# Large tiles laid out anew in on-chip memory, and the first and last copies cut in two, in an attention and gated-MLP kernel

## The chip, the cores and the metric

The kernel runs on one core of a Trainium2 chip. The metric is device time in microseconds (us) of one launch: 688.56 us is the median of three runs of the kernel before (688.14 to 688.83). The engines are named as in the profile: PE is TensorE (matmuls), PEld its weight loads, DVE is VectorE, ACT is ScalarE, POOL is GpSimd, SP issues all the transfers (DMAs).

## What is computed

Attention with a sigmoid in place of the softmax, and behind it a gated MLP whose gate mixes the positions of a sequence. The reference, cut to what matters:

```python
scores = scale * q @ k.T - log(S)          # 8 batches, 12 heads, S = 448, head size 64
attn = sigmoid(scores) @ v                 # heads side by side: x is (8, 448, 768)
h = maximum(x @ w_in, 0)                   # w_in: 768 x 1024
u, v = h[..., :512], h[..., 512:]
v_n = (v - mean(v)) / sqrt(var(v) + 1e-6)  # over the 512 features
v_s = w_spatial @ v_n + b_spatial          # over the 448 positions
out = (u * v_s) @ w_out                    # w_out: 512 x 768
```

## The kernel before

The batches are taken in four pairs (`m` = 0 to 3). For each pair the PE runs, in program order:

- **psc** (`attention_scores`, L237 and L225): scores of one pair of heads. A tile of 128 keys is the stationary operand (the weights, loaded by PEld), 448 queries stream past it. Queries and keys are split into a high and a low float32r part, and three products (`TERMS`) are summed. The short last tile of keys of two units goes in plain float32 (L225, `t == NFULL`). ACT turns the sums into `at` (sigmoid, L245).
- **pav** (`attention_values`, L267): `v` is stationary (64 columns for each of two heads, side by side in the array), `at` streams, in plain float32. The sums are split into the two parts of `x_s`.
- **pv** (`gate_values`): `x_s` is stationary, 512 columns of `w_in_s` stream. Then come the statistics, and the normalised tiles `vn`.
- **pg** (`spatial`): `vn` is stationary, 448 columns of `w_sp_s` stream.
- **pu** (`gated`): the u half of `w_in_s` is stationary, 448 columns of `x_s` stream. The product with the gate is split into two parts, `gs`.
- **po** (`output`): `w_out_s` is stationary, 448 columns of `gs` stream. ACT copies the sums to `osb` (L416) and SP sends them out (L417).

All of pv, pg, pu and po go through one helper, `product` (its matmul is L278), with float32r operands of 128 rows, and each matmul has a weight load of 128 columns of its own. The matmuls of the program number 504 (pv), 352 (pg), 576 (pu) and 576 (po).

Each engine's order is the order of the code (`in_program_order`). Transfers all go through SP's queue in that order: `start_loads` issues the first ones, and `attention` issues the rest a few steps ahead.

Where a tile lies is settled by the pools. A pool lays its tiles one after another in the order of their first use, each rounded up to 32 bytes, with all buffers of a tag together: `small`, then `const` (the weights, `b_bc` and `x_s`), then `work` (`raw`, `v`, `tmp`, `big`, `split`, `wval`). The tile `fill` (608 bytes) is used by nothing; it makes `w_in_s` begin at byte 2048 of each partition. All large tiles have sizes that are multiples of 256 bytes, so before the change all of them begin at multiples of 512.

At the **beginning** PE runs seven matmuls of zeros into `idle` (L478) while the first data come. The first unit's queries and keys come in two transfers (`pieces`): 640 columns with the 128 keys of the first tile, the queries and the short keys, then the 256 other keys. `attention_splits` makes the two parts: ACT copies the 576 columns of the first piece (L103), DVE subtracts (L104); DVE does both for the second. At the **end** the sums of the last two blocks of 128 outputs lie in one tile of two PSUM banks; one copy of 2 x 448 columns and one transfer send them out.

Of the kernel before, what the change touches and what calls it, by code (L numbers as in the profile page):

```python
# [8 lines left out]
F32 = mybir.dt.float32  # L9
F32R = mybir.dt.float32r  # L10
# [4 lines left out]
P = 128  # L15
# [20 lines left out]
def attn_gmlp_kernel(  # L36
# [25 lines left out]
    nc = tc.nc  # L62
    B, NHP, _, _ = qk.shape
    S = out.shape[3]
    D = P // 2
    NCC = out.shape[1]
# [4 lines left out]
    NFULL = 3  # L71

    REST = NFULL * P
    PART = REST + S
# [4 lines left out]
    small = ctx.enter_context(tc.tile_pool(name="small", bufs=2))  # L79
    const = ctx.enter_context(tc.tile_pool(name="const", bufs=1))  # L80
    work = ctx.enter_context(tc.tile_pool(name="work", bufs=2))

    ps_2 = ctx.enter_context(tc.tile_pool(name="ps_2", bufs=3, space=bass.MemoryType.PSUM))
    ps_1 = ctx.enter_context(tc.tile_pool(name="ps_1", bufs=2, space=bass.MemoryType.PSUM))
# [7 lines left out]
    table = small.tile([P, 1], F32, name="table", bufs=1)  # L92
    nc.scalar.activation(table, bias_s, AF.Sigmoid)

    small.tile([P, 152], F32, name="fill", bufs=1)

    w_in_s = const.tile([P, 2 * NCC, 2, F], F32R, name="w_in_s")
    w_out_s = const.tile([P, NFC * DM // 512, 2, 512], F32R, name="w_out_s")
    w_sp_s = const.tile([P, 4, 2, 512], F32R, name="w_sp_s")
    b_bc = const.tile([P, 512], F32, name="b_bc")  # L100
    x_s = const.tile([P, 2, NCC, 2 * S], F32R, name="x_s")
    def split(hi, lo, src, copy):
        copy(hi, src)  # L103
        nc.vector.tensor_sub(lo, src, hi.bitcast(F32))  # L104

    def banks(name):
        return ps_2.tile([P, 2, 512], F32, tag="ps2", name=name)
# [71 lines left out]
    def load_weights(n):  # L179
        for _ in range(n):  # L180
            next(weights, None)

    loaded = {}
    values = {}

    def pieces(b, hp, end):

        cut = REST - P
        return [slice(cut, end), slice(0, cut)] if b == hp == 0 else [slice(0, end)]

    def attention_loads(b, hp):
        raw = work.tile([P, 1024], F32, tag="raw", name=f"raw_{b}_{hp}", bufs=4)[:, : 2 * S]
        for cols in pieces(b, hp, 2 * S):
            nc.sync.dma_start(raw[:, cols], qk[b, hp, :, cols])
        loaded[b, hp] = raw

    def value_loads(b, hp):
        vt = work.tile([P, 2 * NFULL + 1, P], F32, tag="v", name=f"v_{b}_{hp}", bufs=3)
        nc.sync.dma_start(vt, v[b, hp // 2])
        values[b, hp] = vt  # L200

    parts_of = {}

    def attention_splits(b, hp):
        raw = loaded[b, hp]
        s = work.tile([P, 2, PART], F32R, tag="split", name=f"qks_{b}_{hp}", bufs=3)
        for i, cols in enumerate(pieces(b, hp, PART)):
            scalar = b == 1 or b == 0 and hp not in (1, 2) and i == 0
            split(s[:, 0, cols], s[:, 1, cols], raw[:, cols], nc.scalar.copy if scalar else nc.vector.tensor_copy)
        parts_of[b, hp] = s  # L210

    TERMS = ((0, 0), (1, 0), (0, 1))
# [61 lines left out]
    def product(ps, pairs, more=(), start=True, stop=True):  # L274

        ops = [(st(a), mv(c)) for st, mv in pairs for a, c in TERMS] + list(more)
        for i, (st, mv) in enumerate(ops):
            nc.tensor.matmul(ps, st, mv, start=start and i == 0, stop=stop and i == len(ops) - 1)  # L278
# [109 lines left out]
            hidden[b, fc] = gs[:, :, i]  # L388

    sums_of = {}  # L390

    def output(b, es, part=None):

        if not part:
            sums_of[es] = banks(f"po_{b}_{es[0]}")
        po = sums_of[es]
        n = NFC // 2
        for i, e in enumerate(es):

            def weight(a, fc, e=e):  # L400
                block, col = divmod(fc * DM + e * P, 512)
                return w_out_s[:, block, a, col : col + P]

            product(
                po[:, i, :S],
                [
                    (lambda a, fc=fc: weight(a, fc), lambda c, fc=fc: hidden[b, fc][:, c])
                    for fc in (range(NFC) if part is None else range(part * n, (part + 1) * n))
                ],
                start=not part,  # L410
                stop=part != 0,
            )
        if part == 0:
            return
        osb = work.tile([P, 2, 512], F32, tag="tmp", name=f"osb_{b}_{es[0]}", bufs=3)[:, :, :S]
        nc.scalar.copy(osb, po[:, :, :S])  # L416
        nc.sync.dma_start(out[b, es[0] : es[0] + 2].rearrange("e p s -> p e s"), osb)  # L417

    units = [(b, hp) for b in range(B) for hp in range(NHP)]
# [1 line left out]
    def ahead(f, n):  # L421
        if n < len(units):
            f(*units[n])

    def start_loads(m):
        n = m * 2 * NHP
        ahead(attention_loads, n)
        ahead(attention_loads, n + 1)
        ahead(value_loads, n)
        ahead(attention_loads, n + 2)  # L430

    def attention(m):

        first, end = 2 * NHP * m, 2 * NHP * (m + 1)
        waiting = []

        def scores(n, tiles):
            for t in tiles:
                if t == 1:
                    ahead(attention_splits, n + 1)  # L440
                if n + 2 < end and t == NFULL + 1:
                    ahead(attention_splits, n + 2)
                waiting.append((*units[n], t, attention_scores(*units[n], t)))
                if n + 2 < end:
                    if t == 0:
                        ahead(attention_loads, n + 3)
                        ahead(value_loads, n + 2)
                    elif t == NFULL and n + 4 < end:
                        ahead(attention_loads, n + 4)
                if m == 0 and (n > first or t > NFULL) and t != 2:  # L450
                    load_weights(1)

        def sums(n):
            for args in waiting[:n]:
                attention_values(*args)
            del waiting[:n]

        attention_splits(*units[first])
        yield
        for n in range(first, end, 2):  # L460
            for t in range(NFULL):
                scores(n, [t])
                if n == first:
                    yield
            scores(n, [NFULL])
            sums(NFULL + (n > first))
            scores(n, range(NFULL + 1, TILES))
            sums(len(waiting) - NFULL - 1)
        sums(NFULL + 1)

    start_loads(0)
    load_weights(1)

    zeros = work.tile([P, 512], F32R, tag="big", name="zeros", bufs=7)
    nc.vector.memset(zeros.bitcast(F32), 0.0)  # L475
    idle = banks("idle")
    for _ in range(7):
        nc.tensor.matmul(idle[:, 0], zeros[:, :P], zeros, start=True, stop=True)  # L478

    pairs = [(0, 1), (2, 3)]  # L480
    outs = [(0, 1), (2, 3), (4, 5)]
    running = attention(0)
    for m in range(B // 2):
# [14 lines left out]
        for fcs in pairs:  # L498
            spatial(b1, fcs)
            load_weights(BLOCK)  # L500
        start_loads(m + 1)
        for es in outs:
            output(b0, es)
# [14 lines left out]
        for part in range(2):  # L518
            for es in early:
                output(b1, es, part)  # L520
        for es in outs[len(early) :]:
            output(b1, es)
# [53 lines left out]
```

## Time and profile before

| | before |
|---|---|
| median of three runs | 688.56 us |
| time of the profiled execution | 688.86 us |
| its span, first to last instruction | 687.1 us |
| PE busy | 681.0 us (99%), 3839 instructions |
| PEld busy | 504.9 us (73%) |
| DVE, ACT busy | 292.7 us (43%), 241.2 us (35%) |
| DMA | 55.37 MB, mean 81 GB/s |

The profiled execution is one launch with the hardware profiler on. Its time is its span and 1.8 us around it. A float32 matmul stands as two instructions in the profile, so pav counts 768 for 384 products. PE's matmuls are pipelined: the duration of one (365 ns) reaches beyond the start of the next, and what counts is the distance from start to start, which the rows of the chain of waits give when a long piece of one kind is divided by its count.

### The profile page before, as it was taken

Reading aid. Unit: us, or ns where it says so; the run is one execution under the profiler, and the core shown is the slowest. Engines: PE = TensorE matmul, PEld = TensorE weight load, DVE = VectorE, ACT = ScalarE, POOL = GpSimd, SP = SyncE. Lnnn points to the kernel's source line nnn. Section 1 sums busy time; section 2 is a strip of 40 time slices with the busy share of each in tenths; the row PEclk is TensorE's granted clock in tenths of the full one; section 3 lists DMA queues with packets and bytes.
Section 4 is the critical chain, followed back from the end, with each engine's and each line's share of the span. In section 5 each row is a group of like instructions: output and inputs, shape, how many; then the busy total and the mean of one; then the engine's idle time right before and its main releaser. Section 6 shows DMA issues by size and latency. Waiting matters only on the chain.

```text
span 687.1 us, 9085 instructions
## 1 busy us (share of the span) xinstructions
PE 681.0 (99%) x3839; PEld 504.9 (73%) x3839; DVE 292.7 (43%) x469; ACT 241.2 (35%) x284; POOL 18.5 (3%) x36
## 2 busy tenths in 40 slices
PE   9999999999999999999999999999999999999997
PEld 5444789998554488999854458899984555889996
DVE  6999888803143237221233514721223241563010
ACT  6887010112567510011367651011137773101111
POOL 0000010000000001000000001100000000110000
PEclk9999999999999999999999999999999999999999
DMA  8873202230444100003062500000315310000102
GB/s 311 290 259 98 93 1 88 82 135 27 159 136 150 39 1 0 1 28 107 28 204 96 158 28 0 1 1 27 108 55 188 122 41 1 0 1 0 54 28 80
DMA packets 20392, 55.37 MB, mean 81 GB/s; under 512 B 1920, under 2 KB 8192, under 8 KB 20352
## 3 DMA queue, kind: packets, MB, share of 16 engines
q1 hardware_dynamic: 20352, 54.80, 23.4%
q8 instruction: 30, 0.49, 0.3%
q14 instruction: 10, 0.08, 0.0%
HBM read 43.78 MB, written 11.01 MB: 80 GB/s over the span
## 4 chain that ended last, share of the span: by engine, by line
PE 99%; ACT 0%; DVE 0%; issue 0%
PE pav L267 20%; PE po L278 17%; PE pu L278 17%; PE pv L278 17%; PE psc L237 15%; PE pg L278 10%; PE psc L225 3%; PE idle L478 0%; ACT osb L416 0%; DVE zeros L475 0%; DVE bias_s L88 0%; DVE mhalf L90 0%
## 5 line engine op out<-in xcount | busy, mean ns | idle before, releaser
L245 ACT ACTIVATE at<-psc,bias_s 128x896 f32<-128x896 f32 x168 | 158.6, 1008 | 60.8 <-PE psc L237 58.4
L267 PE MATMUL pav<-at,v 128*64 128x448 f32 (+1 forms) x768 | 139.4, 546 | 0.0
L278 PE MATMUL po<-gs,w_out_s 128*128 128x448 f32 x576 | 118.6, 366 | 0.0
L278 PE MATMUL pu<-x_s,w_in_s 128*128 128x448 f32 x576 | 118.0, 365 | 0.0
L278 PE MATMUL pv<-w_in_s,x_s 128*128 128x512 f32 x504 | 115.4, 390 | 0.0
L278 PEld LDWEIGHTS po<-gs,w_out_s 128*128 128x128 f32 x576 | 107.9, 188 | 9.7 <-ACT at L245 0.9
L278 PEld LDWEIGHTS pu<-x_s,w_in_s 128*128 128x128 f32 x576 | 108.2, 188 | 8.5
L278 PEld LDWEIGHTS pv<-w_in_s,x_s 128*128 128x128 f32 x504 | 94.3, 188 | 22.3 <-issue 2.8
L237 PEld LDWEIGHTS psc<-qks 64*128 64x128 f32 x864 | 77.2, 186 | 39.5 <-ACT at L245 15.5
L267 PEld LDWEIGHTS pav<-at,v 128*64 128x64 f32 (+1 forms) x768 | 44.0, 135 | 82.2 <-issue 76.5
L237 PE MATMUL psc<-qks 64*128 64x448 f32 x864 | 103.2, 379 | 0.2
L104 DVE TENSOR_TENSOR x_s<-pav,x_s 128x448 fp32r<-128x448 f32 x48 | 29.6, 623 | 125.6 <-ACT x_s L103 125.6
L278 PE MATMUL pg<-w_sp_s,vn 128*128 128x448 f32 x352 | 72.7, 365 | 0.0
L278 PEld LDWEIGHTS pg<-w_sp_s,vn 128*128 128x128 f32 x352 | 66.1, 188 | 5.4
L378 DVE SCALAR_TENSOR_TENSOR g<-pu,g 128x896 f32<-128x896 f32 x16 | 17.4, 1090 | 121.3 <-PE pu L278 121.3
L416 ACT COPY osb<-po 128x896 f32<-128x896 f32 x24 | 21.8, 907 | 119.9 <-PE po L278 111.7
L103 ACT CAST gs<-g 128x896 fp32r<-128x896 f32 x16 | 15.1, 942 | 129.9 <-DVE g L378 129.9
L104 DVE TENSOR_TENSOR qks<-raw,qks 128x832 fp32r<-128x832 f32 (+2 forms) x49 | 49.3, 1007 | 4.6 <-ACT qks L103 3.2
L298 ACT ACTIVATE rv<-pv 128x1024 f32<-128x1024 f32 (+1 forms) x16 | 14.8, 922 | 100.8 <-PE pv L278 93.0
L103 DVE CAST qks<-raw 128x832 fp32r<-128x832 f32 (+1 forms) x39 | 22.5, 578 | 33.5 <-PE po L278 31.1
L103 ACT CAST x_s<-pav 128x448 fp32r<-128x448 f32 x48 | 25.5, 532 | 29.0 <-PE pav L267 29.0
L302 DVE BATCH_NORM_STATS2 stats<-rv 128x6 f32<-128x512 f32 x28 | 19.0, 679 | 38.6 <-ACT rv L298 38.6
(33 smaller groups left out, 227.7 us busy)
## 6 DMA issues: line engine op xcount, KB each, us to landing
raw<-qk_dram SPq DMA_DIRECT2D x47, 448.0 KB, 4.1
v<-v_dram SPq DMA_DIRECT2D x24, 448.0 KB, 4.6
out_dram<-osb SPq DMA_DIRECT2D x24, 448.0 KB, 2.6
wraw<-w_in_dram SPq DMA_DIRECT2D x12, 512.0 KB, 4.2
wraw<-w_out_dram SPq DMA_DIRECT2D x6, 512.0 KB, 3.8
wraw<-w_sp_dram SPq DMA_DIRECT2D x4, 256.0 KB, 5.0
raw<-qk_dram SPq DMA_DIRECT2D x1, 320.0 KB, 2.9
b_bc<-b_sp_dram SPq DMA_DIRECT2D x1, 256.0 KB, 5.5
```

The lines of the kernel that those rows point to most:

```text
L103: copy(hi, src)
L104: nc.vector.tensor_sub(lo, src, hi.bitcast(F32))
L225: nc.tensor.matmul(psc[odd * HALF : (odd + 1) * HALF, j, :S], raw[rows, PART : PART + HALF], raw[rows, REST:PART], start=True, stop=True,)
L237: nc.tensor.matmul(psc[:, j, :S], s[rows, a, k : k + P], s[rows, e, REST:PART], start=i == 0, stop=i == len(TERMS) - 1,)
L245: nc.scalar.activation(at, psc[:, :, :S], AF.Sigmoid, bias=bias_s, scale=QK)
L267: nc.tensor.matmul(pav[heads, :S], vt[rows, t, heads], at[rows, j], start=start, stop=stop)
L278: nc.tensor.matmul(ps, st, mv, start=start and i == 0, stop=stop and i == len(ops) - 1)
L298: nc.scalar.activation(rv[:, :n], pv[:, :n], AF.Relu)
L302: nc.vector.bn_stats(stats, rv[:, i])
L378: nc.vector.scalar_tensor_tensor(g, pu[:, :, :S], 0.0, g, op0=ALU.max, op1=ALU.mult)
L416: nc.scalar.copy(osb, po[:, :, :S])
```

## The change

**Layout.** The order of the tiles in `const` becomes `w_sp_s`, `x_s`, a filler of 160 bytes, `w_in_s`, `w_out_s`, `b_bc`. `fill` shrinks to 96 bytes. In `work` a filler of 32 bytes (tag `fill_big`) stands ahead of `big` (the tag of `zeros`, `at` and `vn`), and one of 256 bytes (`fill_split`) ahead of `split` (`qks` and `gs`). The fillers are read and written by nothing. The table gives, from the addresses in the two built programs, where the next weights begin against where the columns that stream meanwhile begin, in bytes modulo 256:

| matmuls | weights, columns | before | after |
|---|---|---|---|
| pu | `w_in_s`, `x_s` | 0 | 160 |
| pg | `vn`, `w_sp_s` | 0 | 192 |
| po | `w_out_s`, `gs` | 0 | 224 |
| pv | `x_s`, `w_in_s` | 0 | 96 |
| pav | `v`, `at` | 0 | 224 |
| psc | one tile, `qks` or `raw` | 0 | 0 |

Taken modulo 512, before the change about half of the matmuls of psc, pav, pg, pu and po have 0 and the others 256; all of pv have 0. After it half of pu have 160 and half 416, and so on. After the change `raw`, `v`, `tmp`, `w_in_s` and `w_out_s` begin at 160 modulo 256, `big` and `split` at 192, `x_s` and `w_sp_s` at 0.

**Beginning.** Six idle matmuls instead of seven. For the first unit DVE copies the 128 keys of the first tile, ACT the 448 queries and then the 256 other keys, and DVE subtracts in the order keys, queries, other keys. The first transfer of `v` is cut: tiles 0 to 2 at its old place, tiles 3 to 6 after the third `raw`.

**End.** The last two blocks of outputs get a PSUM tile each from the pool `ps_1`; DVE copies the first and ACT the second, and each has a transfer of its own.

```diff
-    small.tile([P, 152], F32, name="fill", bufs=1)
-
+    small.tile([P, 24], F32, name="fill", bufs=1)
+
+    w_sp_s = const.tile([P, 4, 2, 512], F32R, name="w_sp_s")
+    x_s = const.tile([P, 2, NCC, 2 * S], F32R, name="x_s")
+    const.tile([P, 40], F32, name="fill_w")
     w_in_s = const.tile([P, 2 * NCC, 2, F], F32R, name="w_in_s")
     w_out_s = const.tile([P, NFC * DM // 512, 2, 512], F32R, name="w_out_s")
-    w_sp_s = const.tile([P, 4, 2, 512], F32R, name="w_sp_s")
     b_bc = const.tile([P, 512], F32, name="b_bc")
-    x_s = const.tile([P, 2, NCC, 2 * S], F32R, name="x_s")
...
     def value_loads(b, hp):
         vt = work.tile([P, 2 * NFULL + 1, P], F32, tag="v", name=f"v_{b}_{hp}", bufs=3)
-        nc.sync.dma_start(vt, v[b, hp // 2])
         values[b, hp] = vt
+        if b == hp == 0:
+            nc.sync.dma_start(vt[:, :NFULL], v[b, hp // 2, :, :NFULL])
+        else:
+            nc.sync.dma_start(vt, v[b, hp // 2])
+
+    def rest_of_values(b, hp):
+        nc.sync.dma_start(values[b, hp][:, NFULL:], v[b, hp // 2, :, NFULL:])
...
-        for i, cols in enumerate(pieces(b, hp, PART)):
-            scalar = b == 1 or b == 0 and hp not in (1, 2) and i == 0
-            split(s[:, 0, cols], s[:, 1, cols], raw[:, cols], nc.scalar.copy if scalar else nc.vector.tensor_copy)
+        if b == hp == 0:
+            chunk, rest, query = slice(REST - P, REST), slice(0, REST - P), slice(REST, PART)
+            nc.vector.tensor_copy(s[:, 0, chunk], raw[:, chunk])
+            for cols in (query, rest):
+                nc.scalar.copy(s[:, 0, cols], raw[:, cols])
+            for cols in (chunk, query, rest):
+                nc.vector.tensor_sub(s[:, 1, cols], raw[:, cols], s[:, 0, cols].bitcast(F32))
+        else:
+            scalar = b == 1 or b == 0 and hp not in (1, 2)
+            split(s[:, 0], s[:, 1], raw[:, :PART], nc.scalar.copy if scalar else nc.vector.tensor_copy)
...
+        single = b == B - 1 and es == outs[-1]
         if not part:
-            sums_of[es] = banks(f"po_{b}_{es[0]}")
+            if single:
+                sums_of[es] = [ps_1.tile([P, 512], F32, tag="ps1", name=f"po_{b}_{e}") for e in es]
+            else:
+                po = banks(f"po_{b}_{es[0]}")
+                whole_of[es] = po
+                sums_of[es] = [po[:, i] for i in range(2)]
...
+        if single:
+            for e, p, copy in zip(es, po, (nc.vector.tensor_copy, nc.scalar.copy)):
+                osb = work.tile([P, 2, 512], F32, tag="tmp", name=f"osb_{b}_{e}", bufs=3)[:, 0, :S]
+                copy(osb, p[:, :S])
+                nc.sync.dma_start(out[b, e], osb)
+            return
...
+    work.tile([P, 8], F32, tag="fill_big", name="fill_big", bufs=1)
     zeros = work.tile([P, 512], F32R, tag="big", name="zeros", bufs=7)
+    work.tile([P, 64], F32, tag="fill_split", name="fill_split", bufs=1)
     nc.vector.memset(zeros.bitcast(F32), 0.0)
     idle = banks("idle")
-    for _ in range(7):
+    for _ in range(6):
```

The order changes only at the two ends. First, what DVE runs at the beginning, before the change (the first number behind a tile's name is the batch, the second the unit, the last a running number):

```order
L475 MEMSET zeros_95 128x512
L104 TENSOR_TENSOR qks_0_0_105<-raw_0_0_82,qks_0_0_105 128x576
L103 CAST qks_0_0_105<-raw_0_0_82 128x256
L104 TENSOR_TENSOR qks_0_0_105<-raw_0_0_82,qks_0_0_105 128x256
L103 CAST qks_0_1_123<-raw_0_1_85 128x832
```

And after it:

```order
L505 MEMSET zeros_98 128x512
L215 CAST qks_0_0_108<-raw_0_0_83 128x128
L219 TENSOR_TENSOR qks_0_0_108<-raw_0_0_83,qks_0_0_108 128x128
L219 TENSOR_TENSOR qks_0_0_108<-raw_0_0_83,qks_0_0_108 128x448
L219 TENSOR_TENSOR qks_0_0_108<-raw_0_0_83,qks_0_0_108 128x256
L105 CAST qks_0_1_128<-raw_0_1_86 128x832
```

The copy of the 256 other keys has left DVE for ACT, a copy of 128 keys has come to it, and the subtraction of 576 columns stands as two, of 128 and 448. Second, SP's first transfers, before:

```order
L194 DMA raw_0_0_82<-qk_dram 128x640
L194 DMA raw_0_0_82<-qk_dram 128x256
L194 DMA raw_0_1_85<-qk_dram 128x896
L199 DMA v_0_0_87<-v_dram 128x896
L194 DMA raw_0_2_89<-qk_dram 128x896
L154 DMA wraw_0_91<-w_in_dram 128x1024
```

And after:

```order
L191 DMA raw_0_0_83<-qk_dram 128x640
L193 DMA raw_0_0_83<-qk_dram 128x256
L191 DMA raw_0_1_86<-qk_dram 128x896
L200 DMA v_0_0_88<-v_dram 128x384
L191 DMA raw_0_2_90<-qk_dram 128x896
L205 DMA v_0_0_88<-v_dram 128x512
L156 DMA wraw_0_93<-w_in_dram 128x1024
```

The values' transfer is cut after 384 of 896 columns, and the other 512 have moved behind the third unit's queries and keys, so that all later transfers are issued one issue later. Third, the last rows of PE, before (the last batch is 7; the second number is the first block of outputs):

```order
L278 MATMUL po_7_2_5049<-gs_7_0_4992,w_out_s_78 128x448 x12
L278 MATMUL po_7_4_5062<-gs_7_0_4992,w_out_s_78 128x448 x12
L278 MATMUL po_7_0_5036<-gs_7_2_5033,w_out_s_78 128x448 x12
L278 MATMUL po_7_2_5049<-gs_7_2_5033,w_out_s_78 128x448 x12
L278 MATMUL po_7_4_5062<-gs_7_2_5033,w_out_s_78 128x448 x12
```

And after:

```order
L291 MATMUL po_7_4_5067<-gs_7_0_4997,w_out_s_81 128x448 x6
L291 MATMUL po_7_5_5068<-gs_7_0_4997,w_out_s_81 128x448 x6
L291 MATMUL po_7_0_5041<-gs_7_2_5038,w_out_s_81 128x448 x12
L291 MATMUL po_7_2_5054<-gs_7_2_5038,w_out_s_81 128x448 x12
L291 MATMUL po_7_4_5067<-gs_7_2_5038,w_out_s_81 128x448 x6
L291 MATMUL po_7_5_5068<-gs_7_2_5038,w_out_s_81 128x448 x6
```

The matmuls and their order are the same; blocks 4 and 5 now write a tile each, so the copy of block 4 waits for its own six alone.

More of the change, by code (lines that the diff above doesn't have):

```diff
@@ L184, in attn_gmlp_kernel @@
     values = {}
-    def pieces(b, hp, end):
-        cut = REST - P
-        return [slice(cut, end), slice(0, cut)] if b == hp == 0 else [slice(0, end)]
     def attention_loads(b, hp):
         raw = work.tile([P, 1024], F32, tag="raw", name=f"raw_{b}_{hp}", bufs=4)[:, : 2 * S]
-        for cols in pieces(b, hp, 2 * S):
-            nc.sync.dma_start(raw[:, cols], qk[b, hp, :, cols])
+        cut = REST - P if b == hp == 0 else 0
+        nc.sync.dma_start(raw[:, cut:], qk[b, hp, :, cut:])
+        if cut:
+            nc.sync.dma_start(raw[:, :cut], qk[b, hp, :, :cut])
         loaded[b, hp] = raw
@@ L390, in attn_gmlp_kernel @@
     sums_of = {}
+    whole_of = {}
     def output(b, es, part=None):
+        single = b == B - 1 and es == outs[-1]
         if not part:
-            sums_of[es] = banks(f"po_{b}_{es[0]}")
+            if single:
[4 more added lines that the diff above has]
+                sums_of[es] = [po[:, i] for i in range(2)]
         po = sums_of[es]
@@ L404, in output @@
             product(
-                po[:, i, :S],
+                po[i][:, :S],
                 [
@@ L414, in output @@
             return
+        if single:
[4 more added lines that the diff above has]
+            return
         osb = work.tile([P, 2, 512], F32, tag="tmp", name=f"osb_{b}_{es[0]}", bufs=3)[:, :, :S]
-        nc.scalar.copy(osb, po[:, :, :S])
+        nc.scalar.copy(osb, whole_of.pop(es)[:, :, :S])
         nc.sync.dma_start(out[b, es[0] : es[0] + 2].rearrange("e p s -> p e s"), osb)
@@ L430, in start_loads @@
         ahead(attention_loads, n + 2)
+        if m == 0:
+            rest_of_values(0, 0)
     def attention(m):
```

## Prediction

> **What bounds the kernel now.** I read the page's first part and its chain of work first.
>
> ```profile
> PE 681.0 (99%) x3839; PEld 504.9 (73%) x3839; DVE 292.7 (43%) x469; ACT 241.2 (35%) x284; POOL 18.5 (3%) x36
> ...
> PE 99%; ACT 0%; DVE 0%; issue 0%
> ```
>
> PE is the bound from end to end: 99% of the chain is PE, and nothing that another engine does can be worth more than the last 1%. So only two things can move the time: the distance from one matmul to the next, and the stretches before the first and behind the last real matmul. The chain in order of time gives the distances: a long piece of one kind, divided by its count. Here are four answers, each for a window inside one stage (start, length, kind, count).
>
> ```profile
> 113.85 8.31 PE pu L278 x41
> ...
> 74.85 17.23 PE pv L278 x76
> ...
> 332.80 7.29 PE po L278 x36
> ...
> 162.92 7.23 PE po L278 x35
> ```
>
> A matmul of 448 columns comes every 8.31 / 41 = 202.7 ns in pu and 7.29 / 36 = 202.5 in po; one of 512 columns in pv every 17.23 / 76 = 226.7 ns. The last row is the same po stage for another batch: 7.23 / 35 = 206.6 ns, with the same tiles and columns. So the distance has at least two values that no operand explains. How fast could PE take columns? Two pairs of rows from the timeline tell, pav at full clock and the idle matmuls at the start.
>
> ```profile
> 17.88 2.05 PE L267 MATMUL pav<-at,v 128*64 128x448 f32 x10
> ...
> 17.88 0.92 PE L267 MATMUL pav<-at,v 128*64 128x448 f32 x4
> ...
> 1.50 1.22 PE L478 MATMUL idle<-zeros 128*128 128x512 f32 x2 [1.50 <-DVE zeros L475]
> ...
> 1.50 2.93 PE L478 MATMUL idle<-zeros 128*128 128x512 f32 x6 [1.50 <-DVE zeros L475]
> ```
>
> Six more pav instructions, which run in pairs side by side, take 2.05 - 0.92 = 1.13 us, 376.7 ns a pair. Read as two passes of 448 columns that is 0.4204 ns a column. Four more idle matmuls take 2.93 - 1.22 = 1.71 us, 427.5 ns each or 0.835 ns a column: twice 0.4175, PE at half speed and with no loss at all. Against 0.4204 ns a column, 448 columns need 188.3 ns and lose 202.7 - 188.3 = 14.4 ns, and 512 columns need 215.2 and lose 11.5 ns. The loss is nearly the same for both lengths, so it is a price per matmul, not per column, and what each of them has once is its weight load:
>
> ```profile
> L278 PEld LDWEIGHTS pu<-x_s,w_in_s 128*128 128x128 f32 x576 | 108.2, 188 | 8.5
> ```
>
> It takes 188 ns and runs beside the stream of the matmul before it. That is what the layout edits aim at: two reads of the same memory at the same time.
>
> **The layout edit, part by part.** It adds and removes no work. It changes where the weights read meanwhile lie against the columns that stream: 0 modulo 256 before, for every matmul of the kernel, and 160 (pu), 192 (pg) and 224 (po) after. The trace of before has only that one residue, so it shows no price for another. Bounds come from its rows. The best case is that the whole loss goes: 1504 matmuls of 448 columns (576 + 352 + 576) by 14.4 ns are 21.7 us, and 504 of pv by 11.5 are 5.8, together 27.5 us. The worst that the trace shows is the 206.6 ns of the one po stage: 1504 x 3.9 ns = 5.9 us more. Between them I take the row nearest in kind, pv: the same helper, operand type and weight load, and a loss of 11.5 instead of 14.4 ns. The 2.9 ns by which 448 columns lose more look like waiting for the load of 188 ns, which nearly fills a distance of 202.7 but not one of 226.7. If the new residues shorten what the two reads cost each other a little, these 2.9 ns go first: 1504 x 2.9 = **4.4 us**. For pv itself (now 96) I take nothing, with -5.8 to +2.0 us (504 x 3.9) as its bounds, already in the two sums above. pav (now 224) loses at most 896 x (0.4204 - 0.4175) = 2.6 ns a pair, so it has nothing to win; some 190 pairs by 11.5 ns would be 2.2 us if it came to lose what pv does, which I hold to be unlikely. psc keeps 0: its operands lie in one tile. So psc is the control.
>
> The Trainium skill, page "SBUF — State Buffer", section "Who interferes with whom", gives PE two independent read ports, one for the moving operand and one for weight loads; by that rule no layout can change the distance, and the edit is worth 0. The rows above have a loss of 11.5 to 14.4 ns with a load beside the stream, but no run so far shows whether it comes from the load. The page "TensorE: Matmul & The Clock Gate", section "Back-to-back issue gap", has N/2.4 + 2.5 ns, which is 189.2 and 215.8 ns; the trace has 202.7 and 226.7, and where they differ the trace decides. By that formula the best case would be 1504 x 13.5 + 504 x 10.9 = 25.8 us.
>
> The transfers now write `raw`, `v` and `tmp` at 160 modulo 256. In the first 70 us, the busiest for DMA, PE waits for a transfer once, below; I put this at nothing, covered by PE's 99%.
>
> **The beginning.** The timeline of before, and three forms of the copies:
>
> ```profile
> 1.50 3.35 PE L478 MATMUL idle<-zeros 128*128 128x512 f32 x7 [1.50 <-DVE zeros L475]
> ...
> 3.64 0.67 ACT L103 CAST qks<-raw 128x576 fp32r<-128x576 f32 x1 [1.42 <-DMA raw<-qk_dram]
> ...
> 4.78 3.08 PE L237 MATMUL psc<-qks 64*128 64x448 f32 x18
> ...
> 6.80 0.59 DVE L103 CAST qks<-raw 128x832 fp32r<-128x832 f32 x1 [1.04 <-DMA raw<-qk_dram]
> ...
> 7.79 0.98 PE L225 MATMUL psc<-raw 64*64 64x448 f32 x8
> ...
> 8.71 0.20 PEld L267 LDWEIGHTS pav<-at,v 128*64 128x64 f32 x4 [0.71 <-DMA v<-v_dram]
> ...
> L103 ACT CAST qks<-raw 128x832 fp32r<-128x832 f32 x9 | 8.0, 883 | 0.0
> ...
> L103 ACT CAST qks<-raw 128x576 fp32r<-128x576 f32 x1 | 0.7, 671 | 1.4 <-DMA raw<-qk_dram 1.4
> ...
> L104 DVE TENSOR_TENSOR qks<-raw,qks 128x576 fp32r<-128x576 f32 x1 | 0.8, 759 | 2.9 <-ACT qks L103 2.9
> ```
>
> The first real matmul comes at 4.78. The copy ended at 3.64 + 0.67 = 4.31, and the seventh idle matmul, 427 ns after the sixth, kept PE until about 4.65. After the change ACT copies 448 columns: from 883 and 671 ns, 0.83 ns a column, 565 ns, done at 4.21; the sixth idle matmul ends at 4.22. So the first real matmul starts at about 4.26, 0.52 us earlier. Its third pair needs the low part of the queries, 626 ns on DVE by the same slope (759 ns for 576 columns), done near 4.87, and comes at about 5.2. The other keys are copied by 4.62 and subtracted by 5.3, and are wanted at 5.6 and 5.9. Nothing is late.
>
> The 18 instructions of psc are 9 pairs in 7.79 - 4.78 = 3.01 us, where 9 at 203 ns are 1.8: PE still runs at half speed for most of them (374 ns a pair by the idle rate). If full speed comes at the same moment as before, about 6.9 us, the 0.52 us are work at half speed, worth 0.52 x 203 / 374 = **0.3 us**; if it comes earlier too, 0.5; if an input is late, 0. Late next would be the values (PE waited 0.71 us for them, until 8.71), and of these only 384 of 896 columns are now needed and queued there; the second unit's transfer, which DVE waited for until 6.80, is wanted by PE at 7.5. The rest of `v` is wanted by the fourth tile's product, near 17 us, and the weight transfers go one issue later behind DVE's splits; I cost both at nothing.
>
> **The end.** The last rows of the timeline, the forms for half the size, and the transfers:
>
> ```profile
> 681.98 0.77 PE L278 MATMUL po<-gs,w_out_s 128*128 128x448 f32 x3
> ...
> 682.78 0.91 ACT L416 COPY osb<-po 128x896 f32<-128x896 f32 x1 [1.46 <-PE po L278]
> 683.71 0.37 SPq L417 DMA_DIRECT2D out_dram<-osb  x1
> ...
> L104 DVE TENSOR_TENSOR x_s<-pav,x_s 128x448 fp32r<-128x448 f32 x48 | 29.6, 623 | 125.6 <-ACT x_s L103 125.6
> L103 ACT CAST x_s<-pav 128x448 fp32r<-128x448 f32 x48 | 25.5, 532 | 29.0 <-PE pav L267 29.0
> ...
> out_dram<-osb SPq DMA_DIRECT2D x24, 448.0 KB, 2.6
> ...
> raw<-qk_dram SPq DMA_DIRECT2D x1, 128.0 KB, 2.8
> ```
>
> Behind PE's end at 682.75 stand a copy of 0.91 us, a transfer and the tail of the program, to 687.1. The copy of 448 columns takes 0.53 on ACT, 0.38 less. Block 4 ends its six matmuls 1.2 us earlier, DVE copies it in some 0.62, and its transfer is issued near 682.2, a full microsecond ahead of the other: SP is free. The last transfer has half the bytes. Of its 2.6 us some part is fixed; the 128 KB row (2.8, in the crowd at the start) would leave nothing to win, half of 2.6 would be 1.3; I take 0.6. Together **1.0 us**, bounds 0.4 and 1.7.
>
> **The sum.** 4.4 + 0.3 + 1.0 = 5.7 us. The profiled execution took 688.86 us, the median is 688.56; the difference, 0.3, is the spread of the runs. From the median: **682.9 us**.
>
> **The rivals.** (1) *The layout does nothing*: the loss is of the weight load's hand-over, wherever the bytes lie. For it: 0 and 256 modulo 512 both occur in pu, pg and po, at one and the same distance. Only the ends are left: 688.56 - 1.3 = 687.3, with 686.4 to 688.2 by their bounds. (2) *The whole loss goes*: 688.56 - 1.3 - 27.5 = 659.8. For it: pav and the idle matmuls run with loads beside them and without loss. Against it: the load of 188 ns alone nearly fills 188.3, so something must shorten it too. (3) *Slower*: the new residues put pu, pg and po at the 206.6 ns that one po stage shows. The price is 5.9 us against 1.3 won: 693.2. It decides from 1.3 us / 1504 = 0.9 ns a matmul on. For it: the kernel does fall into that distance, for a whole stage, without a cause that the trace names; against it: once in eight.
>
> **How the numbers follow.** A chance of 0.40 for the forecast (the distance falls by 1 to 8 ns: 675.3 to 685.8), 0.32 for the layout that does nothing, 0.16 for a gain beyond 8 ns up to the whole loss, 0.12 for the slower distance. The range from 671 to 688.6 holds the first two and half of the third: 0.40 + 0.32 + 0.08 = 0.8. A measurement of this kernel can tell about 0.2%, 1.4 us, from no change; the ends alone (1.3) lie on that line, so half of their 0.32 counts as faster. Faster: 0.40 + 0.16 + 0.16 = 0.72. Same: 0.16 and 0.02 of the third rival, where a loss of about 1 ns cancels the ends: 0.18. Slower: 0.10.
>
> **What the profile after would show.** If I am right: pieces of pu, pg and po with some 200 ns a matmul, psc at its old distance, pv near 226.7; the first psc near 4.26 and the float32 psc near 7.5; the last copy 0.53 long and the stretch from PE's last matmul to the end of the span 3.4 instead of 4.4 us. I am wrong if pu, pg and po still stand at 202.7 (rival 1), if they differ among themselves by more than a few ns (then the residue matters, and not only that it isn't 0), or if psc has moved too (then it isn't the meeting of two tiles at all).

## The result, and the profile after

The changed kernel takes 692.85 us (median of four, 692.55 to 693.83) against 688.38 (688.14 to 688.83): 1.0062 times as long, with a 95% interval of 1.005 to 1.0074, so 4.5 us slower by the medians. 682.9 was forecast. The profiled execution took 692.55 us with a span of 690.8.

PE is the bound as before (99% of the chain of waits). Here are the pieces of the chain of waits in the windows of the prediction (start, length, kind, count), for the changed kernel:

```profile
111.87 10.27 PE pu L291 x50
...
74.88 17.34 PE pv L291 x74
...
131.96 13.09 PE po L291 x64
...
333.86 7.23 PE po L291 x35
...
98.94 8.20 PE pg L291 x41
```

For pg, which the prediction did not show apart, the same window before:

```profile
98.85 8.31 PE pg L278 x41
```

From start to start, pv went from 226.7 to 17.34 / 74 = 234.3 ns, pu from 202.7 to 10.27 / 50 = 205.4, po (first batch) from 202.5 to 13.09 / 64 = 204.5; the po stage of batch 3, 202.5 before, now stands at 7.23 / 35 = 206.6. Only pg fell, from 8.31 / 41 = 202.7 to 8.20 / 41 = 200.0. So the layout does change the distance, and in both directions. The whole stages give the sum. Of the four pairs of batches, the first, before:

```profile
69.86 28.79 PE pv L278 x126
98.65 8.92 PE pg L278 x44
107.57 14.59 PE pu L278 x72
...
131.08 14.59 PE po L278 x72
...
668.15 14.60 PE po L278 x72
```

And after:

```profile
68.83 29.71 PE pv L291 x126
98.54 8.81 PE pg L291 x44
107.35 14.79 PE pu L291 x72
...
130.94 14.72 PE po L291 x72
...
672.33 14.88 PE po L291 x72
```

pv costs 0.92 us more in each of its four stages, 3.7 us. pu costs 0.20 more in each of eight, 1.6. pg costs 0.11 less in each of eight, -0.9. po costs 1.2 more over its eight. pv begins 1.03 us earlier, which is the beginning, and behind PE's last matmul stand 690.8 - 687.2 = 3.6 us where 4.35 stood, which is the end. 3.7 + 1.6 - 0.9 + 1.2 - 1.0 - 0.75 is 3.8 to 3.9, and the spans differ by 3.7 us.

The beginning and the end in the timeline after:

```profile
3.76 0.87 ACT L217 CAST qks<-raw 128x448 fp32r<-128x448 f32 x2 [1.55 <-DMA raw<-qk_dram]
3.76 0.23 DVE L215 CAST qks<-raw 128x128 fp32r<-128x128 f32 x1 [2.32 <-DMA raw<-qk_dram]
...
4.38 2.46 PE L250 MATMUL psc<-qks 64*128 64x448 f32 x18
...
6.77 0.98 PE L238 MATMUL psc<-raw 64*64 64x448 f32 x8
...
7.68 0.20 PEld L280 LDWEIGHTS pav<-at,v 128*64 128x64 f32 x4 [0.70 <-issue]
...
685.99 0.62 DVE L438 COPY osb<-po 128x448 f32<-128x448 f32 x1 [10.44 <-PE po L291]
...
686.64 1.53 SPq L439 DMA_DIRECT2D out_dram<-osb  x2
687.27 0.53 ACT L438 COPY osb<-po 128x448 f32<-128x448 f32 x1 [1.56 <-PE po L291]
```

The first real matmul comes at 4.38 instead of 4.78, the float32 scores at 6.77 instead of 7.79, and no load of pav's weights is put down to a wait for `v`. PE itself lost nothing to `v` in the profile before: from its last float32 score to the first pav it took 465 ns there and 466 ns here. The two copies take 0.62 and 0.53 us, as taken from before's rows.

### The profile page after: what moved, and what is told of

Its sections match the earlier page's. It is cut to its first block, busy times and chain, and to the rows that moved or that the text cites. A ratio compares the mean times of both kernels' runs of the same rounds, so it can differ in the third digit from the quotient of the medians.

```text
span 690.8 us, 9090 instructions
## 1 busy us (share of the span) xinstructions
PE 685.4 (99%) x3838; PEld 504.1 (73%) x3838; DVE 293.7 (43%) x471; ACT 240.8 (35%) x285; POOL 18.5 (3%) x36
## 4 chain that ended last, share of the span: by engine, by line
PE 99%; DVE 0%; ACT 0%; issue 0%; ACTq 0%
PE pav L280 19%; PE pv L291 17%; PE po L291 17%; PE pu L291 17%; PE psc L250 14%; PE pg L291 10%; PE psc L238 3%; PE idle L508 0%; ACT osb L438 0%; DVE zeros L505 0%; DVE bias_s L88 0%; DVE mhalf L90 0%; ACTq L438 0%
## 5 line engine op out<-in xcount | busy, mean ns | idle before, releaser
L291 PE MATMUL pu<-x_s,w_in_s 128*128 128x448 f32 x576 | 119.6, 368 | 0.0
L291 PE MATMUL pv<-w_in_s,x_s 128*128 128x512 f32 x504 | 119.1, 397 | 0.0
L106 DVE TENSOR_TENSOR qks<-raw,qks 128x832 fp32r<-128x832 f32 x47 | 48.1, 1024 | 1.5 <-ACT qks L105 0.2
L105 DVE CAST qks<-raw 128x832 fp32r<-128x832 f32 x38 | 22.3, 587 | 33.1 <-PE po L291 31.5
```

## The experiments

The experiments ask which half of the change costs the time, whether it is where two tiles meet or where each of them lies, and which residue costs what; the last one asks which two reads collide. In what follows a residue is the start of the weights minus the start of the columns, modulo 256.

**The ends alone.** The changed kernel with the layout of before:

```diff
-    small.tile([P, 24], F32, name="fill", bufs=1)
+    small.tile([P, 152], F32, name="fill", bufs=1)
...
-    const.tile([P, 40], F32, name="fill_w")
...
-    work.tile([P, 8], F32, tag="fill_big", name="fill_big", bufs=1)
-    work.tile([P, 64], F32, tag="fill_split", name="fill_split", bufs=1)
```

(with the tiles of `const` in their old order.)

> The change's two ends with the layout of before. Theory A (the layout alone made the kernel slower; the ends gain as drawn): pu, pg, po 202.7 ns and pv 226.7 ns from start to start, as before; between 1.1 us faster (end 0.75, start 0.3 as forecast) and 1.8 us faster (end 0.75, start 1.0 as in the profile after), so 686.6 to 687.3 us. Theory B (the ends, by another phase at the start, set the distances between matmuls): the distances move as in the profile after, pv to 234 ns, and the time is above 691 us.

Measured: 687.7 us against 688.92, 0.9981 times (0.9972 to 0.999), 1.3 us faster. (Here and below a gain or loss in us is this ratio times the time before.) In the chain pv, pg and pu are as before:

```profile
69.91 28.79 PE pv L289 x126
98.70 8.92 PE pg L289 x44
107.62 14.59 PE pu L289 x72
```

Theory A holds: together the ends are worth what was forecast, and they don't touch the distances.

**The layout alone.** The kernel before with the changed kernel's tile order and fillers (the first and the last hunk of the diff, and still seven idle matmuls).

> The change's layout with the two ends of before. Theory A: pv 234.3, pu 205.4, pg 200.1, po 204.4 ns, psc and pav as before; 504 x 7.6 + 576 x 2.7 - 352 x 2.6 + 576 x 1.8 = 5.5 us slower, about 693.9 us. Theory B: the distances of before and 688.4 us.

Measured: 694.44 against 688.92, 1.0078 times (1.0065 to 1.0091), 5.4 us slower; -1.3 and +5.4 make 4.1 of the 4.5 us of the whole. The pieces of the first pair of batches have the lengths of the changed kernel to 0.01 us:

```profile
69.82 29.71 PE pv L280 x126
99.53 8.81 PE pg L280 x44
108.33 14.79 PE pu L280 x72
...
131.92 14.72 PE po L280 x72
```

**Everything moved together.** The one edit to the kernel before is the size of a filler:

```diff
-    small.tile([P, 152], F32, name="fill", bufs=1)
+    small.tile([P, 192], F32, name="fill", bufs=1)
```

> The kernel before with every large tile moved by 160 bytes together: all of them begin at 160 modulo 256, and weights and columns still meet at 0. Theory M (what counts is where the weights lie against the columns that stream meanwhile): the distances of before, 202.7 and 226.7 ns, and the time of before within 0.3%. Theory T (what counts is each tile's own place; 160 is no multiple of 64, and in the profile after the stages with a tile at 160 were the ones that became slower): pv at 234 ns or above, pu and po at 205 ns or above, 693 us or more.

Measured, a single execution: 688.59 against 688.92, and every distance as before:

```profile
69.45 28.78 PE pv L278 x126
98.24 8.92 PE pg L278 x44
107.15 14.59 PE pu L278 x72
...
130.66 14.59 PE po L278 x72
```

Theory T falls. It had fitted the profile after: the three stages with a tile at 160, which is no multiple of 64, were the slower ones. But with all tiles at 160 nothing changes, so what counts is how weights and columns lie against each other.

**pv alone.** The kernel before, with the changed kernel's order of tiles and `w_in_s` cut into a tile for each half, so that pv meets at 96 and all else at 0:

```diff
-    w_in_s = const.tile([P, 2 * NCC, 2, F], F32R, name="w_in_s")
+    const.tile([P, 40], F32, name="fill_wv")
+    w_v_s = const.tile([P, NCC, 2, F], F32R, name="w_v_s")
+    const.tile([P, 24], F32, name="fill_wu")
+    w_u_s = const.tile([P, NCC, 2, F], F32R, name="w_u_s")
```

> The kernel before with w_in_s cut into two tiles, so that pv alone meets at 96 and all others at 0. Theory M (each kind of matmul pays for its own residue): pv 234.3 ns, pu, pg and po as before, 504 x 7.4 = 3.7 us slower. If the price at 96 came from what the layout did to other tiles, pv stays at 226.9 ns and the time at that of before.

Measured: 692.07 against 688.71, 1.0047 times (1.0031 to 1.0063), 3.2 us slower where 3.7 was expected, and pv has the length that it has in the changed kernel. So pv pays for its own residue, and this is the greatest part of the loss:

```profile
69.85 29.72 PE pv L283 x126
99.57 9.09 PE pg L283 x44
108.66 14.88 PE pu L283 x72
...
270.92 8.91 PE pg L283 x44
279.84 14.60 PE pu L283 x72
```

The rows also show the second value that the prediction had met in one po stage: for the first pair of batches pg and pu take 9.09 and 14.88 us (206.6 ns a matmul), for the second 8.91 and 14.60, at the same addresses. The first pair keeps the second value through five stages on end (pg, pu, pg, po, pu), 304 matmuls by 4 ns or 1.2 us, and loses it behind the scores that come next. If the timed executions lack it, which no trace shows, that is most of why they took 692.03 to 692.08 us and the profiled one 693.48.

**A scan of the residues.** Six kernels, all the kernel before with the changed kernel's order of tiles and other fillers, give the other residues; their times are of single executions. The edit, for the second of the six, against the layout alone:

```diff
-    const.tile([P, 40], F32, name="fill_w")
+    const.tile([P, 8], F32, name="fill_w")
...
-    work.tile([P, 64], F32, tag="fill_split", name="fill_split", bufs=1)
+    work.tile([P, 32], F32, tag="fill_split", name="fill_split", bufs=1)
```

| fillers of `w_in_s`, `big`, `split`, bytes | pu | pg | po | pv | us, before beside it |
|---|---|---|---|---|---|
| 128, 224, 128 | 128 | 96 | 160 | 128 | 694.09, 688.92 |
| 32, 32, 128 | 32 | 64 | 96 | 224 | 691.21, 689.32 |
| 64, 160, 64 | 64 | 224 | 32 | 192 | 690.63, 689.32 |
| 192, 224, 96 | 192 | 160 | 192 | 64 | 689.84, 689.32 |
| 224, 64, 128 | 224 | 32 | 64 | 32 | 694.07, 689.32 |
| 96, 32, 96 | 96 | 128 | 128 | 160 | 691.10, 688.71 |

> The kernel before with other fillers: residues (weights minus columns, modulo 256) pu 128, pv 128, pg 96, po 160. Theory M with one function of the residue for all matmuls of 448 columns: po stands at 205.4 ns, where pu stood at 160 in the profile after; nothing known for pu and pg. Theory T: pu and pv, all of whose tiles begin at multiples of 64, as before at 202.7 and 226.7 ns; pg (weights at 96) and po (columns at 224) slower by 2 to 8 ns.

> Residues pu 32, pv 224, pg 64, po 96. Theory M with one function of the residue modulo 256 for all matmuls of 448 columns: po at 96 takes one of the two values of pg at 96 (206.7 or 200.0 ns); pu and pg unknown, between 199 and 207 ns; pv between 226 and 235 ns. Theory M2 (modulo 512): po shows 206.7 ns where the residue is 96 and 200.0 where it is 352, within one stage.

> Residues pu 64, pv 192, pg 224, po 32. Theory M with one function: po as pu at 32 in the run before this, pu as pg at 64 there, pg at 204.4 ns as po at 224 in the profile after; pv between 226 and 235 ns.

> Residues pu 192, pv 64, pg 160, po 192. Theory M with one function: pu and po at 200.1 ns, as pg at 192 in the profile after, and pg at 205.4 ns, as pu at 160; pv (64) between 226.7 at 0 and 234.3 at 96, some 231 ns if the price grows evenly. If pg, pu and po have a function each, pu and po stay near 205.

> Residues pu 224, pv 32, pg 32, po 64. Theory M with one function: pu at 204.4 ns, as po at 224 in the profile after; pg as pu and po at 32, po as pu and pg at 64 in the other runs of this scan; pv (32) some 229 ns if the price grows evenly from 0 to 96.

> The last points of the scan: residues pu 96, pv 160, pg 128, po 128. One function for all matmuls of 448 columns: pg and po at 204.0 ns, as pu at 128; pu at 200.1 or 206.7, as po and pg at 96; pv unknown, between 228.9 (192) and 232.3 (128) if neighbours tell. If the function were smooth, pu would lie between 202.2 (64) and 204.0 (128).

The chain of waits of each gives the lengths of the stages. Divided by 72 (pu, po) and 44 (pg) they are, in ns, with pv's whole stage of 126 matmuls in us. The changed kernel's own residues are in the table too. A second figure is that of other batches in the same execution. The po stages that begin behind scores are left out, because their first and last steps make them 0.2 us longer; the 206.6 of the first row is from the prediction's window (7.23 / 35):

| residue | pu | pg | po | pv stage, us |
|---|---|---|---|---|
| 0 (before) | 202.6 | 202.7 | 202.6, 206.6 | 28.79 |
| 32 | 204.3, 203.2 | 204.3 | 204.4 | 29.60 |
| 64 | 202.1 | 202.3 | 202.2 | 29.60 |
| 96 | 200.4 | 206.4, 200.0 | 200.3 | 29.71 |
| 128 | 204.0 | 203.9 | 203.9 | 29.47 |
| 160 | 205.4 | 205.2 | 205.3 | 29.60 |
| 192 | 200.0 | 200.2 | 200.0 | 29.06 |
| 224 | 206.5 | 206.1, 200.0 | 204.4, 206.7 | 29.60 |

The row of 192 rests on these pieces, of the fourth kernel (pu and po at 192, pg at 160, pv at 64):

```profile
70.06 29.60 PE pv L280 x126
99.66 9.03 PE pg L280 x44
108.69 14.40 PE pu L280 x72
...
132.12 14.40 PE po L280 x72
```

Three kinds of matmuls with different tiles agree at 0, 32, 64, 128, 160 and 192 within 0.5 ns for the first batches: one function of the residue, as theory M has it. It is not smooth: in pu and po 96 and 192 lie lowest, at 200 ns, and between them 128 and 160 at 204 and 205. At 96 and 224, as at 0 in po, a second value of 206 to 207 ns occurs, so there the residue alone does not settle the distance. In pg the two values go with the batch, in all four pairs, here at 224 (the third kernel):

```profile
99.31 9.07 PE pg L280 x44
...
122.94 8.80 PE pg L280 x44
```

The even and the odd batch differ in two ways: their columns begin 256 bytes apart, and the even one's pg comes behind pv, the odd one's behind pu. No run separates the two. The 256 bytes alone are not enough for it: pu's columns differ by them too, and its two batches agree within 0.4 ns at every residue but 32 (1.1 ns). The expectation that po shows both values of pg at 96 within one stage (M2, modulo 512) failed: po stays near 200 ns for both residues there. The guess that pv's price grows evenly from 0 to 96 failed too: it has most of its price, 0.81 of 0.92 us a stage, at 32. For pv 0 is the best of the eight, and every other residue costs at least 0.27 us a stage.

**The change mended.** The changed kernel with pu and pv back at 0 and the two that can move at 192:

```diff
-    const.tile([P, 40], F32, name="fill_w")
...
-    work.tile([P, 8], F32, tag="fill_big", name="fill_big", bufs=1)
+    work.tile([P, 48], F32, tag="fill_big", name="fill_big", bufs=1)
...
-    work.tile([P, 64], F32, tag="fill_split", name="fill_split", bufs=1)
+    work.tile([P, 32], F32, tag="fill_split", name="fill_split", bufs=1)
```

> The changed kernel with three fillers changed: w_in_s and w_out_s begin at 0, vn 192, gs 64. Residues pu 0, pv 0, pg 192, po 192. Theory M: pu 202.7, pv 226.9, pg and po 200.0 ns: 352 x 2.7 + 576 x 3.1 = 2.7 us less than before, and 1.2 for the ends as measured apart: 3.9 us faster than before, some 684.6 us where before has 688.5. If the residues were no lasting property of the meeting, the time of the ends alone, 687.3 us.

Measured: 685.07 against 688.71, 0.9943 times (0.9929 to 0.9957), 3.9 us faster at that ratio (the medians differ by 3.6), as expected. The first pair's stages are as expected too: 28.80 us for pv, 8.80 for pg, 14.60 for pu and 14.41 for po.

**All at their best.** On top of it `w_in_s` is cut in two, with the u half 192 bytes past, so that pu leaves 0 and pv does not; the fillers behind it are set so that pg and po stay at 192:

```diff
-    w_in_s = const.tile([P, 2 * NCC, 2, F], F32R, name="w_in_s")
+    w_v_s = const.tile([P, NCC, 2, F], F32R, name="w_v_s")
+    const.tile([P, 48], F32, name="fill_wu")
+    w_u_s = const.tile([P, NCC, 2, F], F32R, name="w_u_s")
```

> As the repair, and w_in_s cut into two tiles, so that the u half can begin at 192 while the v half stays at 0. Residues pu, pg, po 192, pv 0. Theory M: another 576 x 2.7 = 1.6 us, together 5.5 us faster than before, some 683 us.

Measured: 683.01 against 688.71, 0.9918 times (0.9905 to 0.9931), 5.7 us faster where 5.5 was expected: the fastest of all kernels here. That this is next to the 682.9 forecast for the change is chance; it is another layout.

```profile
69.88 28.79 PE pv L293 x126
98.67 8.80 PE pg L293 x44
107.47 14.40 PE pu L293 x72
...
130.67 14.40 PE po L293 x72
```

**Own weights or the next ones?** The kernel before with `x_s` cut into a tile for even and one for odd blocks, the odd one at 96, so that in pv a matmul's own weights and those loaded beside it differ at every third:

```diff
-    x_s = const.tile([P, 2, NCC, 2 * S], F32R, name="x_s")
+    x_even = const.tile([P, 2, NCC // 2, 2 * S], F32R, name="x_even")
+    const.tile([P, 24], F32, name="fill_x")
+    x_odd = const.tile([P, 2, NCC // 2, 2 * S], F32R, name="x_odd")
```

> The kernel before with x_s cut into two tiles, for even and for odd blocks, the odd one at 96: in pv the weights begin at 0 for three matmuls and at 96 for the next three, in turn, while the columns stay at 0. Theory N (what counts is the next weights, read while the columns of the matmul before them stream): of each six distances the long ones, 234 ns, are those whose next weights begin at 96, the last even one among them, and the last odd one is short, 226.9. Theory O (what counts is a matmul's own weights): the last even one is short and the last odd one long. Either way pv has 230.6 ns on average, and pu (0 and 160) 204.

Measured, a single execution: 692.72 us against 688.71. Both theories fall. Sorted by own and next residue, and without the first step of each stage, the mean distances in the trace are 231.4 (0 and 0), 231.5 (0 and 96), 231.2 (96 and 0) and 232.6 ns (96 and 96), where each theory has 226.9 for some of them: matmuls that see 0 alone are slower too. pu, half of it at 0 and half at 160, does not mix either:

```profile
69.30 29.40 PE pv L283 x126
...
107.78 14.79 PE pu L283 x72
```

14.79 / 72 = 205.4 ns is the value of 160 alone, where 204 was expected. So a matmul's distance isn't settled by its own residue and the next one. The starts in the other traces say so too. Single distances repeat in short cycles: in pv of the changed kernel 231, 238, 237, 231, 234, 235, 234 ns, over and over, where before stood an even 226 to 227; in pu of the kernel before 199, 207, 202, 203, 202. The operands come in threes (`TERMS`) and in products of 18, and neither is a multiple of seven or five. Which reads collide, if it is reads that collide, stays open.

## Why the prediction was wrong

- **What bounds the kernel** held: PE's distances and the two ends are all that moved, and their sum closes on the difference of the spans within 0.1 us.
- **The step that failed is the price of the new residues.** The trace of before has one residue, and I took the nearest row in kind, pv's loss, for what pu, pg and po would come to: "these 2.9 ns go first", 4.4 us won. In its place stand 1.6 + 1.2 - 0.9 = 1.9 us lost. pg did fall as drawn (200.0 ns), and so do pu and po at 192. But the change has pu at 160 and po at 224, and these are above 0 and not below: +2.7 and +1.8 ns and more, where -2.9 was forecast. The forecast took all residues other than 0 as one case; the scan shows that it matters which. The prediction had this as a sign of being wrong ("if they differ among themselves by more than a few ns"), and it came: 205.4, 200.0 and 204.5 ns. Whether the 2.9 ns are a wait for the load of 188 ns, as I took them to be, no run shows.
- **pv was the larger miss.** "For pv itself (now 96) I take nothing", with +2.0 us as the upper bound. It costs 3.7 us, 7.6 ns a matmul, two thirds of the 5.4 us that the layout alone costs. The bound was another stage's row (206.6 against 202.7), and there was no ground for a second value of one length to limit the price of a new residue for another. Nor is this +2.0 "already in the two sums", as the prediction says: the 5.9 us are of the other 1504 matmuls alone. The reason why pv is hit was in the tables: pu and pv meet with the same two tiles the other way round, so with 160 for the one goes 96 for the other, and 504 of the 2008 matmuls paid for a choice that was named for pu.
- **Rival 1** (the layout does nothing) fell with the run of the layout alone. Its support, 0 and 256 modulo 512 at one distance, is true and only says that these two residues are alike. The Trainium skill's rule on the page "SBUF — State Buffer", section "Who interferes with whom", that PE's moving operand and its weight loads have independent ports, does not carry so far that their places are free: they move the distance here by up to 7.6 ns.
- **Rival 2** (the whole loss goes) is not seen at any residue: the lowest values, 200.0 and 226.7 ns, still lie 11.7 and 11.5 ns above the pace of pav. These two are nearly alike: once the 2.9 ns are gone, both lengths lose the same.
- **Rival 3** named the right side and nearly the number (693.2), by luck: it had a second value for pu, pg and po, all of them. The second value does occur more often (in three of the eight po stages instead of one), but it carries little; pv, which the rival left out, carries most.
- **The ends** were right in sum: 1.3 us forecast, 1.3 measured with the layout of before (0.7 to 1.9 by the interval). The end gave 0.75 for 1.0. The beginning gave 1.0 in the profile after where 0.3 was drawn, and nothing in the profile of the ends alone, where pv begins at 69.91. Over all profiles pv begins at 68.83 to 69.91 us with the new beginning (four kernels, 69.55 on average) and at 69.28 to 70.25 with the old one (eleven, 69.79). That fits the 0.3, but the spread is too wide to show it; the moment at which PE comes to full speed, below, and in some profiles a wait for `v` move it more. The 0.71 us that the prediction read as PE's wait for the values were idle time of the weight loads: PE's own step there was 465 ns, as without a wait.
- **psc as control** held: its tiles meet at 0 throughout, and it kept its distance: a piece of 24 of its instructions takes 2.80 us before and 2.79 after.

## What to carry to other kernels

When matmuls follow each other without a wait and each loads weights, look at the distance from start to start, in tenths of a ns over a long stage, and then at where weights and columns begin against each other: here the start of the one minus the start of the other, modulo 256 bytes, was worth up to 4 us of 689 for one kind of matmuls. Write down the residue of every pair of tiles that meet, those too which an edit moves without naming them; two products that use the same two tiles the other way round can't both be placed unless one tile is cut. Where a trace has one value of a quantity only, it bounds no other value; a scan with fillers measures the others.

## What the runs showed of the hardware

- The distance of float32r matmuls here depends on the residue of weights against columns: 200.0 to 206.6 ns for 448 columns, and 28.79 to 29.71 us for a stage of 126 matmuls of 512, in a scan by steps of 32 bytes. 256 bytes more or less make at most 0.4 ns in pu at all residues but 32; for pg at 96 and 224 the period is open. The places themselves don't matter as far as tried: the whole layout moved by 160 bytes kept every distance. Plain float32 matmuls (pav) kept theirs through all the layouts: the longest piece of the chain, 32 instructions, takes 5.72 us in all fifteen profiles.
- At one residue there can be two distances, 202.7 and 206.6 ns at 0, with the same tiles. A stage keeps one of them, and stages that follow each other without a break can hand it on. The upper value is nearly the same at 0, 96 and 224, with even steps of 206 to 207 ns in the traces. What chooses between them is open.
- PE comes to full speed at another moment in each profile, by its steps: a pair of scores comes every 373 ns at first and every 203 or so later, while the granted clock stands at 1.00 even at the idle matmuls of half speed (the profile before, 2.0 to 4.6 us). The nine pairs from the first scores to the float32 scores took 3.01 us before and 6.77 - 4.38 = 2.39 in the profile after, and in that of the ends alone 7.91 - 4.36 = 3.55:

```profile
4.36 3.62 PE L248 MATMUL psc<-qks 64*128 64x448 f32 x18
7.91 0.98 PE L236 MATMUL psc<-raw 64*64 64x448 f32 x8
```

In the eleven profiles with the beginning of before they take 2.11 to 3.39 us. That is more than the beginning was recast for, so one profile does not show what such an edit is worth.
